# Attention and two feed-forward blocks in one launch: three of the four large products cut into 2x2 blocks and done in seven products, the norm moved ahead of its product, and the whole program ordered by a list scheduler

## The chip, the core and the metric

The kernel runs on one core of a Trainium2 chip. The core has a matrix engine (TensorE, PE in the tables; its weight loads are PEld), a vector engine (VectorE, DVE), a scalar engine (ScalarE, ACT), GpSimd (POOL), and a queue for DMAs (SyncE, SP). Each engine works through its own list of instructions in order and waits on semaphores for the others. Matrix products are gathered in PSUM, eight banks of 128 x 512 float32; the rest lies in SBUF. The metric is the device time in microseconds, a median over runs.

## The reference

```python
scores = scale * q @ k.T                      # 2 x 12 heads, 448 x 448, head size 64
attn   = softmax(where(causal, scores, -1e9))
x  = attn @ v                                 # 896 tokens x 768
h  = x @ w_in                                 # 768 x 2048            "in1"
g  = where(h >= 1, h, where(h <= -1, 0, (h + 1)**2 / 4))
y  = g @ w_out                                # 2048 x 768            "out1"
xn = y / sqrt(mean(y*y) + 1e-6) * rms_g       # per token
a  = silu(xn @ w_gate) * (xn @ w_val)         # 768 x 1536, twice     "gate/val"
return a @ w_out2                             # 1536 x 768            "out2"
```

The weights come as float64. The host passes them on as pairs of 32-bit words, and the kernel makes a float32 of each pair.

## The kernel before, in words

Everything is kept transposed: features on the 128 partitions, tokens along the columns. The 896 tokens are two batches of S = 448, and h = 0, 1 stands for the batch from in1 on. Attention works through 12 groups of two heads (`scores`, `maxima`, `exps`, `transposes`, `pv`, `xsplit`), with TensorE going through scores, transposes and PV products of neighbouring groups in turn.

Every operand of a large product is split into a high part (rounded to the matrix engine's fast 32-bit format) and a low part (the rest), and a product is three matmuls: high x high, high x low, low x high (`mm3`, L371; out1 at L564; out2 at L679). Each matmul is 128 x 128 weights by 128 x 448 tokens. So in1 is 16 column blocks x 2 batches x 6 x 3 = 576 matmuls, out1 576, gate/val 2 x 12 x 2 x 6 x 3 = 864, out2 6 x 2 x 12 x 3 = 432.

A weight block of 128 x 768 goes through a pipeline of steps: a DMA of 768 KB into one of three staging buffers (L139), a scaling on ScalarE (L174, `w_scale`), a shift, an `or` of the sign and a combining `or` on VectorE (L159, L165, L178), the high part on ScalarE (L184), the low part on GpSimd (L192). From the seventh block on the partial words lie in two PSUM banks. The paces at which these steps are put among the others are the six numbers of `RATE`; `w_need` forces what is due.

After in1, `moe_act` and `moe_min` (L379, L380, L384) make g. `gsplit` (L517, L518) splits it for out1, two blocks ahead. After out1, `rms_a` takes the six result blocks from PSUM: y times rms_g, split (L579, L581), and the squares (L580), summed (L584). The sum over features is a matmul against ones (L590), and the reciprocal root R follows (L591 to L601). The normalisation itself is done behind gate and val: their results are multiplied by R on the way out of PSUM (L642, L644), then SiLU (L643) and the product (L645), and `split` (L631, L632) for out2. The order of the instructions on every engine is that of the code, a schedule written by hand: while attention's last three units run, `push_in` and `pump` put two column blocks of in1 (36 matmuls) into the gaps.

```python
for k in ks:
    for n, (a, c) in enumerate(((0, 0), (0, 1), (1, 0))):
        nc.tensor.matmul(out, lhsT=w[:, a, k * P:(k + 1) * P], rhs=x[:, c, k], ...)   # L371
```

## Time and profile before

| | |
|---|---|
| time, median of 3 runs | 609.89 us (609.83 to 610.97) |
| span of the profiled execution | 607.9 us |
| between span and median | 2.0 us |
| busy: TensorE, VectorE, ScalarE, GpSimd | 594.1, 391.0, 281.9, 173.0 us |
| matmuls and transposes | 3124 |
| DMA | 67.8 MB, 112 GB/s over the span |

The span runs from the first to the last instruction of the profiled execution; the time of a run has some 2 us around it. Busy time is the sum of what an engine's instructions last. TensorE's matmuls overlap: one lasts about 0.37 us in the profile, and they start 0.2 us apart.

### The profile page before, as it was taken

How to read it: one execution, taken by the hardware profiler on the slowest of the kernel's cores; microseconds unless marked ns; L12 is line 12 of the kernel's file. 1: busy time of each engine (PE TensorE's matmuls, PEld its weight loads, DVE VectorE, ACT ScalarE, POOL GpSimd, SP SyncE). 2: the span in 40 equal slices, each digit the busy share in tenths (PEclk: the TensorE clock that was granted, in tenths of full speed). 3: DMA queues.
4: the chain of work that ended last, by engine and by line, in shares of the span. 5: the costliest groups of instructions: out<-in, count | busy, mean ns of one | idle time of the engine just before them, and what ended most of it. 6: DMA issues, size and time to landing. Idle time of an engine off the chain costs nothing.

```text
span 607.9 us, 8305 instructions
## 1 busy us (share of the span) xinstructions
PE 594.1 (98%) x3124; PEld 517.8 (85%) x3124; DVE 391.0 (64%) x643; ACT 281.9 (46%) x555; POOL 173.0 (28%) x118
## 2 busy tenths in 40 slices
PE   6999999899999999999999999999999999999997
PEld 4555558799999989998899999999999999999996
DVE  5678884378787646655594688877767766963100
ACT  5778775266676644345434433333333333543100
POOL 3446442234334413230122103322222222232200
PEclk9999999899999999999999999999999999999999
DMA  8454541234554423431132203333332333182100
GB/s 305 125 172 118 165 115 30 69 104 157 160 187 173 158 72 134 145 116 52 53 104 85 72 1 105 104 110 132 123 105 104 105 105 104 53 250 89 42 31 30
DMA packets 21495, 67.81 MB, mean 112 GB/s; under 512 B 5264, under 2 KB 11408, under 8 KB 21456
## 3 DMA queue, kind: packets, MB, share of 16 engines
q1 hardware_dynamic: 21456, 67.30, 34.1%
q8 instruction: 24, 0.39, 0.3%
q14 instruction: 15, 0.12, 0.1%
HBM read 64.49 MB, written 2.80 MB: 111 GB/s over the span
## 4 chain that ended last, share of the span: by engine, by line
PE 96%; DVE 1%; ACT 1%; issue 1%; DMA 0%; POOL 0%; SPq 0%; ACTq 0%; DVEq 0%
PE ps L371 48%; PE ps L564 18%; PE ps L679 14%; PE ps L278 7%; PE ps L309 4%; PE ps L352 4%; DMA af<-in_qT 0%; PE ps L590 0%; DVE ar L581 0%; ACT af L379 0%; ACT af L380 0%; ACT af L293 0%; DVE ps L165 0%; DVE af L178 0%; ACT af L327 0%
## 5 line engine op out<-in xcount | busy, mean ns | idle before, releaser
L371 PE MATMUL ps<-ar 128*128 128x448 f32 x1440 | 294.4, 367 | 0.0
L371 PEld LDWEIGHTS ps<-ar 128*128 128x128 f32 x1440 | 271.2, 189 | 22.0 <-issue 0.6
L192 POOL TENSOR_TENSOR ar<-af,ar 128x768 fp32r<-128x768 f32 x68 | 128.6, 1892 | 329.7 <-ACT ar L184 329.6
L564 PE MATMUL ps<-ar 128*128 128x448 f32 x576 | 118.1, 366 | 0.4 <-DVE ar L581 0.3
L564 PEld LDWEIGHTS ps<-ar 128*128 128x128 f32 x576 | 108.0, 188 | 10.2 <-DVE ar L581 0.9
L184 ACT CAST ar<-af 128x768 fp32r<-128x768 f32 x68 | 60.3, 887 | 99.1 <-DVE af L178 96.2
L679 PE MATMUL ps<-ar 128*128 128x448 f32 x432 | 87.7, 365 | 0.0
L679 PEld LDWEIGHTS ps<-ar 128*128 128x128 f32 x432 | 81.2, 188 | 6.4
L174 ACT ACTIVATE af<-af 128x768 f32<-128x768 f32 x62 | 56.6, 913 | 26.4 <-DMA af<-in_w_out 16.3
L165 DVE SCALAR_TENSOR_TENSOR ps<-af,ps 128x768 int32<-128x768 int32 x62 | 59.6, 961 | 12.2 <-ACT af L174 9.7
L159 DVE TENSOR_SCALAR ps<-af 128x768 int32<-128x768 int32 x62 | 59.1, 954 | 5.8 <-DMA af<-in_w_out 4.8
L178 DVE SCALAR_TENSOR_TENSOR af<-af,ps 128x768 int32<-128x768 int32 x62 | 59.2, 954 | 5.2
L293 ACT ACTIVATE af<-ps,nm 112x336 f32<-112x336 f32 (+2 forms) x96 | 47.0, 504 | 14.6 <-DVE nm L285 13.4
L285 DVE CUSTOM_DVE_ANT_0 ps<-ps,af 112x336 f32<-112x336 f32 (+2 forms) x96 | 41.8, 466 | 17.0 <-PE ps L278 16.0
L278 PE MATMUL ps<-af 64*112 64x448 f32 (+3 forms) x192 | 42.7, 444 | 7.1 <-DVE af L256 4.5
L518 DVE TENSOR_TENSOR ar<-af,ar 128x448 fp32r<-128x448 f32 x32 | 23.3, 732 | 40.3 <-ACT ar L517 40.3
L384 DVE SCALAR_TENSOR_TENSOR af<-af,ps 128x448 f32<-128x448 f32 x32 | 19.7, 618 | 40.3 <-ACT af L380 40.3
L517 ACT CAST ar<-af 128x448 fp32r<-128x448 f32 x32 | 18.0, 566 | 49.7 <-PE ps L564 49.7
L278 PEld LDWEIGHTS ps<-af 64*112 64x112 f32 x192 | 18.5, 179 | 22.5 <-ACT af L293 6.8
L379 ACT ACTIVATE af<-ps,half 128x448 f32<-128x448 f32 x32 | 20.2, 632 | 27.4 <-PE ps L371 24.9
L682 ACT COPY af<-ps 128x448 f32<-128x448 f32 x12 | 6.4, 533 | 53.4 <-PE ps L679 27.3
L644 DVE TENSOR_TENSOR af<-ps,af 128x448 f32<-128x448 f32 x24 | 14.9, 621 | 24.7 <-PE ps L371 24.7
(49 smaller groups left out, 393.5 us busy)
## 6 DMA issues: line engine op xcount, KB each, us to landing
af<-in_w_out SPq DMA_DIRECT2D x28, 768.0 KB, 4.3
af<-in_w_in SPq DMA_DIRECT2D x16, 768.0 KB, 4.4
af<-in_w_gate SPq DMA_DIRECT2D x12, 768.0 KB, 4.3
...
```

What stands on the lines that cost most here:

```text
L159: nc.vector.tensor_scalar(out=out, in0=t, scalar1=29, scalar2=0, op0=ALU.logical_shift_right, op1=ALU.bitwise_or)
L165: nc.vector.scalar_tensor_tensor(out=t, in0=words(n, 1, I32), scalar=-2 ** 31, in1=t, op0=ALU.bitwise_and, op1=ALU.bitwise_or)
L174: nc.scalar.mul(c, c, 2.0 ** -112)
L178: nc.vector.scalar_tensor_tensor(out=words(n, 0, I32), in0=words(n, 1, I32), scalar=3, in1=part.pop(n), op0=ALU.logical_shift_left, op1=AL ...
L184: nc.scalar.copy(dst[:, 0, :], value(n))
L192: nc.gpsimd.tensor_tensor(out=dst[:, 1, :], in0=value(n), in1=b32(dst[:, 0, :]), op=ALU.subtract)
L278: nc.tensor.matmul(bs[j][:C, o:o + (c + 1) * C], lhsT=q[r, c * C:(c + 1) * C], rhs=k[r, :(c + 1) * C], start=True, stop=True, skip_group_c ...
L285: nc.vector.tensor_tensor_reduce(out=t, in0=t, in1=mask[:C, S - (c + 1) * C:], scale=-1.0, scalar=3e38, op0=ALU.add, op1=ALU.min, accum_ou ...
L293: nc.scalar.activation(Pn[:C, j, poff[c]:poff[c] + w], sbank[n][j][:C, o:o + w], ACTF.Exp, bias=nm[:C, j, c:c + 1], scale=-1.0, accum_out= ...
L371: nc.tensor.matmul(out, lhsT=w[:, a, k * P:(k + 1) * P], rhs=x[:, c, k], start=(k == 0 and n == 0), stop=(k == NK - 1 and n == 2))
L564: nc.tensor.matmul(ybs[dm][:, :S], lhsT=w[:, a, dm * P:(dm + 1) * P], rhs=t[:, c], start=(n == 0 and i == 0), stop=(n == NM - 1 and i == 2))
L679: nc.tensor.matmul(ob[:, :S], lhsT=w2[dm][:, kk // NK, a, kk % NK], rhs=x[:, c], start=(kk == 0 and i == 0), stop=(kk == NF - 1 and i == 2))
```

## The change

**Seven products.** A product of 2x2 blocks needs eight block products. The change does in1, gate/val and out2 in seven, by mixing blocks first. In in1 and gate/val a group takes two weight blocks of 128 columns (`src1`, `src2`, block columns 1 and 2); the first and the second half of the 768 features are the block rows, and the two batches are the block columns of the tokens. Four mixed weights (`add(5)`, `add(6)`, `add(7)`, `add(3)`) and four mixed token blocks (`operand`) are formed in float32, then each of the seven is split into high and low. A group is 7 x 3 x 3 = 63 matmuls where it was 72. Partial sums are shared: a finished product is copied on ScalarE from its bank to a second bank, to which the next product adds (`seeds`), or, for the first groups, summed on VectorE (`sums`). out2 (`outer`) mixes the blocks of `a` and of w_out2 in the same way, with the seven products one after the other. out1 stays plain.

**Normalised first.** `y_out` takes y times rms_g out of PSUM unsplit; `normal` forms R as before and multiplies the tokens by it; only then are they mixed and split. Gate and val come out of PSUM with no factor.

**One scaling and sign step.** The scaling on ScalarE becomes a leaky form that leaves sign and exponent in place; VectorE's separate sign step is gone, and the shift stays in SBUF.

**Order.** Nothing is issued when it is described. Each operation goes into `Plan` with the engines that may do it, a duration on each, and what it reads and writes. `run` gives each a latest start, counted back from TensorE's sequence, and places them by that; an operation without a PSUM operand can go to VectorE or GpSimd, and one of VectorE marked as sharing with GpSimd is not placed beside one of GpSimd. TensorE's order is fixed by the code (`chain`). The table of durations (`act_t`, `dve_t`, `pool2_t`) sets the order; two of its entries stand below. Buffers are handed out from two arenas by which was freed first, and in the attention part at most two weight blocks are staged, later three.

```diff
+        order = sorted(range(n), key=lambda i: (lst[i], i))
+        lines = {e: [] for e in self.ENGINES}
...
+        self.start, self.end, self.eng = start, end, eng
+        for i in sorted(range(n), key=lambda i: (start[i], i)):
+            self.fn[i](eng[i])
+
+
+def act_t(n, bias=False):
+    return 0.03 + 0.001 * n + (0.06 if bias else 0.0)
+
+
+def dve_t(n):
+    return 0.07 + 0.00105 * n
...
-    def w_sign(n):
-        if wide:
-            t = part[n]
-            nc.vector.scalar_tensor_tensor(out=t, in0=words(n, 1, I32), scalar=-2 ** 31, in1=t,
-                                           op0=ALU.bitwise_and, op1=ALU.bitwise_or)
...
+        top = ("top", st.off, len(plan.alts))
+        low = ("low", st.off, len(plan.alts))
+        op({"ACT": act_t(n)},
+           lambda e: nc.scalar.activation(words(1, F32), words(1, F32), ACTF.Prelu, scale=2.0 ** -112,
+                                          alpha=-2.0 ** 32), [st], [top])
+        op({"DVE": (dve2_t(n), True)},
+           lambda e: nc.vector.tensor_scalar(out=words(0, I32), in0=words(0, I32), scalar1=29, scalar2=0,
+                                             op0=ALU.logical_shift_right, op1=ALU.bitwise_or), [st], [low])
...
+    def group(src1, src2, T, out, need, seeded, ps, rel=(0.0, 0.0), leads=(16, 10, 8)):
...
+        def mix_ps():
+            room([HW] * 4, W7)
+            w_float(st[0], True, None)
+            add(5, q(21), q(22), ALU.add)
+            raw(1)
+            add(6, me(5), q(11), ALU.subtract)
+            add(7, q(11), q(21), ALU.subtract)
+            raw(2)
+            add(3, q(12), me(6), ALU.subtract)
+            free(wf[1].sub(0, HW))
+            raw(4)
+            free(wf[1].sub(HW, HW))
+            for p in sorted(mixed, key=lambda p: need[p]):
+                split(W[p], mixed[p], HW)
+                free(mixed[p])
...
+        def seeds(p, o):
+            if p == 1:
+                bank_of["b"] = n = bank_take()
+                copy_op(bank(n), bank(o), S, [], [bk(o), bk(n)])
+            elif p == 6:
+                bank_of["e"] = n = bank_take()
+                copy_op(bank(n), bank(o), S, [], [bk(o), bk(n)])
+                tmp["u"] = u = SF.first(S, SHORT, ())
+                copy_op(ap(u), bank(o), S, [], [bk(o), u])
+            elif p == 7:
+                u = tmp["u"]
+                tt_op(ap(u), bank(o), ap(u), ALU.subtract, S, [], [bk(o), u], ps=True)
+            elif p == 5:
+                out(22, (o, tmp["u"]))
+                free(tmp["u"])
+            else:
+                out({2: 11, 4: 21, 3: 12}[p], (o, None))
+                bank_give(o)
+
...
+    def group_seq(n, lead_in):
+
+        if lead_in == 2:
+            s = [(0, 1), (1, 1), (0, 2), (1, 2), (0, 5), (1, 5), (0, 6), (1, 6), (0, 7), (1, 7), (0, 4), (1, 4),
+                 (0, 3)]
+            last = 1
+        else:
+            s = [(0, 1), (1, 1), (0, 2), (2, 1), (1, 2), (2, 2)] + [(g, p) for p in (5, 6, 7, 4, 3) for g in range(3)]
+            s.pop()
+            last = 2
+        for g in range(lead_in, n):
+            s += [(g, 1), (last, 3), (g, 6), (g, 2), (g, 7), (g, 5), (g, 4)]
+            last = g
+        return s + [(last, 3)]
...
+    def normal(b):
+        acc = rms[b][0]
+        o = 7
+        op({"PE": 0.95}, lambda e: nc.tensor.matmul(bank(o), lhsT=ap(ones), rhs=ap(acc), start=True, stop=True,
+                                                    skip_group_check=True), [acc, ones], [bk(o)], chain="PE", tail=0.15)
+        ms, rs, R = acc, SF.first(S, SHORT, ()), SF.first(S, SHORT, ())
+        op({"DVE": dve_t(S)}, lambda e: nc.vector.tensor_scalar(
+            out=ap(ms), in0=bank(o), scalar1=1.0 / (NK * P), scalar2=1e-6, op0=ALU.mult, op1=ALU.add), [bk(o)], [ms])
+        op({"ACT": act_t(S) + 1.3}, lambda e: nc.scalar.activation(ap(rs), ap(ms), ACTF.Sqrt), [ms], [rs])
+        for c in range(NCH):
+            x = rs.sub(c * C, C)
...
+            tt_op(ap(x), ap(x), ap(R), ALU.mult, S, [x, R], [x])
+        for p in ((1, 2), (5, 6, 7, 4, 3))[b]:
+            for k in range(HK):
+                ready.add((p, k))
```

The order on the engines, at three places. First TensorE, from the last PV product of attention to the end of the program. L352 and L852 are the PV products, L371 is in1 and gate/val, L564 out1, L590 the matmul against ones, L679 out2. Before:

```order
L352 MATMUL ps<-af 64x112 x2
L352 MATMUL ps<-af 64x336 x2
L352 MATMUL ps<-af 64x224 x2
L352 MATMUL ps<-af 64x112 x2
L371 MATMUL ps<-ar 128x448 x540
L564 MATMUL ps<-ar 128x448 x360
L590 MATMUL ps<-af,ones 128x448
L564 MATMUL ps<-ar 128x448 x216
L371 MATMUL ps<-ar 128x448 x36
L590 MATMUL ps<-af,ones 128x448
L371 MATMUL ps<-ar 128x448 x828
L679 MATMUL ps<-ar 128x448 x432
```

After (L491 in1 and gate/val, L1026 out1, L980 the matmul against ones, L561 out2):

```order
L852 MATMUL ps<-sf 64x112 x2
L491 MATMUL ps<-sr 128x448 x504
L1026 MATMUL ps<-sr 128x448 x306
L980 MATMUL ps<-sf 128x448
L1026 MATMUL ps<-sr 128x448 x270
L491 MATMUL ps<-sr 128x448 x9
L980 MATMUL ps<-sf 128x448
L491 MATMUL ps<-sr 128x448 x747
L561 MATMUL ps<-sr 128x448 x378
```

The rows of in1 have 504 matmuls in place of 540 and the 36 that stood ahead of this piece; gate/val 756 in place of 864; out2 378 in place of 432. The second matmul against ones has moved from behind 36 matmuls of gate/val to behind 9.

Second VectorE, at the head of gate/val, from the mean of the second batch's squares (L591 before, L983 after) on. Before (L642, L644 and L645 take gate and val out of PSUM; L596 is the reciprocal; L599 to L601 finish R):

```order
L591 TENSOR_SCALAR af<-ps 128x448
L642 TENSOR_TENSOR af<-ps,af 128x448
L644 TENSOR_TENSOR af<-ps,af 128x448
L645 TENSOR_TENSOR af<-af 128x448
L632 TENSOR_TENSOR ar<-af,ar 128x448
L596 RECIPROCAL af<-af 128x112 x4
L599 TENSOR_TENSOR af<-af 128x448
L600 SCALAR_TENSOR_TENSOR af<-af 128x448
L601 SCALAR_TENSOR_TENSOR af<-af 128x448
L642 TENSOR_TENSOR af<-ps,af 128x448
L644 TENSOR_TENSOR af<-ps,af 128x448
```

After (L304 is every two-input operation: `sf` and `sr` are the SBUF arenas, `ps` is PSUM; an output in `sr` is a low part; L349 is the shift of the words):

```order
L983 TENSOR_SCALAR sf<-ps 128x448
L304 TENSOR_TENSOR sr<-sf,sr 128x384
L304 TENSOR_TENSOR sf<-ps,sf 128x384
L304 TENSOR_TENSOR sr<-sf,sr 128x384
L349 TENSOR_SCALAR sf<-sf 128x768
L988 RECIPROCAL sf<-sf 128x112 x4
L304 TENSOR_TENSOR sf<-sf 128x448
L990 SCALAR_TENSOR_TENSOR sf<-sf 128x448
L992 SCALAR_TENSOR_TENSOR sf<-sf 128x448
L304 TENSOR_TENSOR sf<-sf 128x448 x5
L304 TENSOR_TENSOR sr<-sf,sr 128x448
```

Between the matmul against ones and the first low part of the second batch's tokens there now stand the mean, four reciprocals, R, and the products with R on VectorE; before, R was needed only behind the products, on the way out of PSUM.

Third VectorE in the middle of gate/val. Before, two weight blocks' worth of rows (L159, L165 and L178 are the steps of the words):

```order
L159 TENSOR_SCALAR ps<-af 128x768
L165 SCALAR_TENSOR_TENSOR ps<-af,ps 128x768
L178 SCALAR_TENSOR_TENSOR af<-af,ps 128x768
L642 TENSOR_TENSOR af<-ps,af 128x448
L644 TENSOR_TENSOR af<-ps,af 128x448
L645 TENSOR_TENSOR af<-af 128x448
L632 TENSOR_TENSOR ar<-af,ar 128x448
L159 TENSOR_SCALAR ps<-af 128x768
L165 SCALAR_TENSOR_TENSOR ps<-af,ps 128x768
L178 SCALAR_TENSOR_TENSOR af<-af,ps 128x768
```

After (L349 and L359 are the steps of the words):

```order
L304 TENSOR_TENSOR sr<-ps,sr 128x384
L304 TENSOR_TENSOR sf<-sf 128x384
L304 TENSOR_TENSOR sf<-sf,ps 128x384
L304 TENSOR_TENSOR sf<-ps,sf 128x448 x2
L304 TENSOR_TENSOR sr<-ps,sr 128x384
L304 TENSOR_TENSOR sf<-ps,sf 128x448
L349 TENSOR_SCALAR sf<-sf 128x768
L304 TENSOR_TENSOR sf<-ps,sf 128x448
L304 TENSOR_TENSOR sf<-ps,sf 128x384
L359 SCALAR_TENSOR_TENSOR sf<-sf 128x768
L304 TENSOR_TENSOR sr<-sf,sr 128x384
```

Operations of 384 columns, many of them with both inputs in SBUF, have come between the steps of the words, and the low parts of the weights, which GpSimd made before, stand on VectorE.

## Rows read from the trace of the kernel before

**Rows 1.** The page: busy time, share of the span, instructions by engine.
```profile
PE 594.1 (98%) x3124; PEld 517.8 (85%) x3124; DVE 391.0 (64%) x643; ACT 281.9 (46%) x555; POOL 173.0 (28%) x118
```

**Rows 2.** Windows: length; busy PE, PEld, DVE, ACT, POOL; granted clock, DMA share, GB/s.
```profile
0.00:95.00 95.00, 87.93 (x620) 52.62 (x620) 73.18 (x244) 69.99 (x229) 42.50 (x46) 1.00 0.53 163
...
98.80:221.60 122.80, 121.05 (x601) 110.91 (x601) 78.26 (x97) 69.71 (x105) 43.98 (x25) 0.99 0.39 131
221.60:341.00 119.40, 118.37 (x579) 108.23 (x578) 74.98 (x95) 53.36 (x82) 28.25 (x15) 1.00 0.28 93
341.00:517.00 176.00, 176.00 (x869) 162.83 (x868) 130.57 (x165) 61.30 (x91) 40.28 (x22) 1.00 0.30 99
517.00:604.50 87.50, 87.44 (x432) 80.72 (x430) 32.10 (x39) 23.23 (x38) 16.25 (x9) 1.00 0.26 83
```

**Rows 3.** The chain that ended last, after attention: start, us, what.
```profile
110.82 110.76 PE ps L371 x540
...
296.26 1.02 PE ps L590 x2
297.27 43.77 PE ps L564 x216
...
348.34 0.75 PE ps L590 x2
349.09 167.80 PE ps L371 x828
516.89 87.57 PE ps L679 x432
604.52 0.53 ACT af L682
```

**Rows 4.** Timeline at the end of attention: start, us, instruction, [idle before, releaser].
```profile
108.25 2.57 PE L352 MATMUL ps<-af 112*64 112x336 f32 x20 [1.75 <-ACT af L327]
```

**Rows 5.** Groups by shape: line engine op, shapes, count, busy us, mean ns, idle before.
```profile
L184 ACT CAST ar<-af 128x768 fp32r<-128x768 f32 x68 | 60.3, 887 | 99.1 <-DVE af L178 96.2 <-PE ps L371 2.9
L178 DVE SCALAR_TENSOR_TENSOR af<-af,ps 128x768 int32<-128x768 int32 x62 | 59.2, 954 | 5.2
L174 ACT ACTIVATE af<-af 128x768 f32<-128x768 f32 x62 | 56.6, 913 | 26.4 <-DMA af<-in_w_out 16.3 <-DMA af<-in_w_in 10.0
L645 DVE TENSOR_TENSOR af<-af 128x448 f32<-128x448 f32 x24 | 25.5, 1064 | 5.2 <-ACT af L643 3.4
L327 ACT COPY af<-ps 112x448 f32<-112x448 f32 x48 | 24.1, 537 | 9.0 <-PE ps L309 9.0
L644 DVE TENSOR_TENSOR af<-ps,af 128x448 f32<-128x448 f32 x24 | 14.9, 621 | 24.7 <-PE ps L371 24.7
L631 ACT CAST ar<-af 128x448 fp32r<-128x448 f32 x24 | 12.6, 564 | 26.7 <-DVE af L645 26.7
```

**Rows 6.** Single lines: count, duration least/median/greatest in ns, first and last start.
```profile
L159 DVE TENSOR_SCALAR af<-af x4: 543/558/566, 11.1 to 81.1; 128x768 int32<-128x768 int32 x4
L364 POOL TENSOR_TENSOR ar<-af,ar x12: 1127/1930/2342, 25.0 to 119.8; 128x448 fp32r<-128x448 f32 x12
L192 POOL TENSOR_TENSOR ar<-af,ar x68: 1857/1885/2398, 27.4 to 569.4; 128x768 fp32r<-128x768 f32 x68
L645 DVE TENSOR_TENSOR af<-af x24: 624/931/1931, 352.3 to 522.4; 128x448 f32<-128x448 f32 x24
```

**Rows 7.** Timeline in gate/val: start, us, instruction, [idle before, releaser].
```profile
349.67 0.61 DVE L642 TENSOR_TENSOR af<-ps,af 128x448 f32<-128x448 f32 x1
350.20 0.61 DVE L644 TENSOR_TENSOR af<-ps,af 128x448 f32<-128x448 f32 x1
...
354.09 2.98 DVE L596 RECIPROCAL af<-af 128x112 f32<-128x112 f32 x4
...
365.03 1.88 POOL L192 TENSOR_TENSOR ar<-af,ar 128x768 fp32r<-128x768 f32 x1 [25.16 <-ACT ar L184]
...
365.46 1.92 DVE L645 TENSOR_TENSOR af<-af 128x448 f32<-128x448 f32 x1 [0.43 <-ACT af L643]
```

More of the change, by code (lines that the diff above doesn't have):

```diff
@@ new lines, with ap, free, bank @@
+    plan = Plan()
+    op = plan.op
+    E = {"PE": nc.tensor, "ACT": nc.scalar, "DVE": nc.vector, "POOL": nc.gpsimd, "SP": nc.sync}
+    def ap(b, dtype=None):
+        t = b.space.tile[:, b.off:b.off + b.n]
+        return t if dtype is None else t.bitcast(dtype)
+    def free(*bufs):
+        for b in bufs:
+            b.space.free(b)
+    def bank(i):
+        return pst[:, i, :S]
+    def bk(i):
+        return BANK + i
+    ident = SF.alloc(P)
+    ones = SF.alloc(P)
+    half = SF.alloc(1)
@@ new lines, with bank_take, bank_give, copy_op @@
+    gvec = SF.alloc(NK)
+    stats = [SF.alloc(3 * 2 * NCH) for _ in range(4)]
+    bfree = {i: 0 for i in range(8)}
+    bclock = [0]
+    def bank_take():
+        i = min(bfree, key=lambda i: bfree[i])
+        del bfree[i]
+        return i
+    def bank_give(i):
+        bclock[0] += 1
+        bfree[i] = bclock[0]
+    def copy_op(dst, src, n, r, w, **kw):
+        op({"ACT": act_t(n)}, lambda e: nc.scalar.copy(dst, src), r, w, **kw)
+    def tt_op(dst, a, b, alu, n, r, w, ps=False, pool=True, **kw):
+        alts = {"DVE": (dve_t(n), not ps)}
+        if not ps and pool:
+            alts["POOL"] = pool2_t(n)
+        op(alts, lambda e: E[e].tensor_tensor(out=dst, in0=a, in1=b, op=alu), r, w, **kw)
@@ L367, in mm3 @@
-    def mm3(out, w, x, ks=None):
-        ks = range(NK) if ks is None else ks
-        for k in ks:
-            for n, (a, c) in enumerate(((0, 0), (0, 1), (1, 0))):
-                nc.tensor.matmul(out, lhsT=w[:, a, k * P:(k + 1) * P], rhs=x[:, c, k],
-                                 start=(k == 0 and n == 0), stop=(k == NK - 1 and n == 2))
-    ntmp = [0]
-    def moe_act(m, h, ps):
-        u = tmp[ntmp[0] % 2]
-        ntmp[0] += 1
-        nc.scalar.activation(u, ps, ACTF.Relu, bias=half, scale=0.5)
-        nc.scalar.activation(u, u, ACTF.Square)
-        gate.append((m, h, ps, u))
@@ new lines, with moe_out, out @@
+    half_a = ap(half)
+    def moe_out(G, j):
+        def out(qn, src):
+            o, t = src
+            g = G[qn, j] = SF.first(S, LONG, ())
+            u = SF.first(S, SHORT, ())
+            h, hk = bank(o), bk(o)
+            if t is not None:
+                tt_op(ap(g), h, ap(t), ALU.add, S, [t], [hk, g], ps=True)
+                h, hk = ap(g), g
+            op({"ACT": act_t(S, True)},
+               lambda e: nc.scalar.activation(ap(u), h, ACTF.Relu, bias=half_a, scale=0.5), [], [hk, u])
+            op({"ACT": act_t(S)}, lambda e: nc.scalar.activation(ap(u), ap(u), ACTF.Square), [u], [u])
+            op({"DVE": (dve_t(S), t is not None)}, lambda e: nc.vector.scalar_tensor_tensor(
+                out=ap(g), in0=ap(u), scalar=1.0, in1=h, op0=ALU.min, op1=ALU.max), [u], [hk, g])
+            free(u)
+        return out
@@ new lines, in val_out, with out @@
+    def val_out(j):
+        def out(qn, src):
+            o, u = src
+            t = A[qn, j] = sil[qn, j]
+            if u is not None:
+                h = SF.alloc(S)
+                tt_op(ap(h), bank(o), ap(u), ALU.add, S, [u], [bk(o), h], ps=True)
+                tt_op(ap(t), ap(h), ap(t), ALU.mult, S, [h, t], [t])
+                free(h)
+            else:
+                tt_op(ap(t), bank(o), ap(t), ALU.mult, S, [t], [bk(o), t], ps=True)
+        return out
+    NL = NF // 2
+    srcs, outs = [], []
@@ L685 @@
+    emit_preps(-3, 5)
+    free(*held)
+    staged[1] = 3
+    for i in range(6):
+        bank_give(i)
+    for i, f in enumerate(units):
+        now[0] = i
+        while later and later[0][0] <= i:
+            later.pop(0)[1]()
+        emit_preps(i, i)
+        f()
+    body = tc.manual_schedule()
+    body.__enter__()
+    plan.run()
     body.__exit__(None, None, None)
@@ L700, with words @@
     wide = w_in.dtype == np.float64
+    def words(w):
+        return w.view(np.int64) if wide else w
     def blocks(w):
[L703 to L704 removed]
+        w = words(w)
         K, N = w.shape
```

1241 lines of the change are left out of this document (810 added, 431 removed).

## The prediction

> **What bounds the kernel now.** I read the busy shares first, then the stages in a table of windows, then the chain that ended last. TensorE is busy 594.1 of 607.9 us, VectorE 391.0, ScalarE 281.9 [rows 1]. In the table of windows TensorE fills every stage after attention (121.05 of 122.80 us, 118.37 of 119.40, 176.00 of 176.00, 87.44 of 87.50), while VectorE has 122.80 - 78.26, 119.40 - 74.98, 176.00 - 130.57 and 87.50 - 32.10 us to spare [rows 2]. The chain says the same in order of time: long unbroken pieces of matmul and hardly anything between [rows 3]. A busy TensorE need not be one at its best, so I take its pace from the chain: 828 matmuls in 167.80 us, 432 in 87.57, 216 in 43.77 are 202.7, 202.7 and 202.6 ns each; the first 540 took 110.76 us, 205.1 ns each, in a stretch whose windows show the granted clock at 0.99 [rows 2, 3]. So today the time is the number of matmuls times 202.7 ns, plus attention, plus the end. Any change in it must come from fewer matmuls or from a new wait of TensorE.
>
> The span is 607.9 us and the median of the runs 609.89, so 2.0 us lie around the span; I sum against the span and add the 2.0 at the end.
>
> **What the change removes.** The listed order of TensorE has 2448 matmuls of 128x448 before (576 + 36 + 828 in the blocks that share L371, 576 in out1, 432 in out2) and 2214 after (504 in in1, 576 in out1, 756 in gate/val, 378 in out2). That the change does what it says is thereby settled before any run: 234 fewer, times 202.7 ns, are 47.4 us. Attention's matmuls and transposes are the same, in the same order.
>
> The sum from the left: in1 works unbroken from 110.82 us on and had put 36 matmuls into gaps of attention before that [rows 3], so without them it would stand at 110.82 - 36 x 0.2027 = 103.5 us. These 36 covered waits: the last PV product waited 1.75 us for a copy on ScalarE [rows 4], behind in1's own Relu and Square. After the change nothing of in1 stands there, TensorE waits in the open, but the copy also comes sooner; I take 103.5, from 102.5 to 105.5. Then 2214 x 0.2027 = 448.8 us; two matmuls against the ones for the norm, 1.02 + 0.75 = 1.8 [rows 3]; the end from the last matmul to the end of the span, 607.9 - 604.5 = 3.4, unchanged but for a VectorE subtraction in place of a ScalarE copy. That is 557.5 us with no new wait. The same reckoning for the kernel before gives 103.5 + 2448 x 0.2027 + 1.8 + 3.4 = 604.9, so it has 3.0 us of waits and clock; they are the measure of what a good order loses.
>
> **What it adds.** Each product of the seven needs its own weights and tokens, mixed by additions and split into a high and a low part. The pieces are 384 columns wide in place of 768, a width that the trace does not have. A VectorE operation takes 0.621 us at 448 columns and 0.954 at 768 [rows 5], a straight line between them gives 0.55 at 384; the bounds are 0.53 (in proportion) and 0.62. ScalarE takes 0.564 at 448 and 0.887 at 768, so 0.50 at 384 (0.48 to 0.564). GpSimd's two-input form at its quickest takes 1.127 us at 448 and 1.857 at 768 [rows 6], so 0.98 at 384; its slowest at 448 columns, 2.342, is the upper end. Copies from one PSUM bank to another, which seed the later products, are priced as a copy out of PSUM, 0.537 [rows 5] (up to 0.954, what an operation of 768 columns takes). The new way to turn the 64-bit words into floats saves a pass: one ScalarE operation as before (0.913), a shift that now stays in SBUF (0.558 instead of 0.954 [rows 5, 6]) and one combination (0.954): 68 times 0.954 + 0.40 less on VectorE.
>
> VectorE in all, counted from the listed order: 250 operations of 384 columns at 0.55, 282 of 448 at 0.62, 15 and 68 of 768 at 0.95, 68 shifts at 0.56, 6 us of reciprocals, and attention's own, some 75 (73.2 in its first 95 us [rows 2], with its weight passes taken off and its last group put on): 137 + 175 + 79 + 38 + 6 + 75 = 510 us. That is 91% of 558 us where it was 64%. ScalarE comes to about 435 us, 78%. These are durations; two neighbours that don't wait for each other start 0.53 us apart where each lasts 0.61 to 0.62 [rows 7], so VectorE's need is some 0.08 us less for each of these 680 or so operations, about 455 us.
>
> By stage, because the mean means little. In in1, TensorE needs 504 x 0.2027 = 102.2 us; VectorE has 174 operations in that part of its order, 106.9 us by durations and 93 by starts; ScalarE 98 and 82. In gate/val a group of two weight blocks is 63 matmuls, 12.8 us, and VectorE needs for it 2 shifts, 2 combinations, 11 operations of 384 and 4 of 448 columns on average: 11.5 by durations, 10.1 by starts. In out2 it is 94 and 82 us against 76.6 us of TensorE, but a fifth of these stand in gate/val's time. Out1 has slack. So TensorE stays the bound if VectorE's queue runs as in [rows 7], and VectorE is late by up to 5 us in in1 if every duration counts in full. The order is one fixed list per engine, and a late operation holds all behind it on its engine; what protects TensorE is that weights are made 8 to 16 products ahead.
>
> The new waits that I can place: (1) The norm of the second batch. Its matmul against the ones runs one product after out1, and then five products (45 matmuls, 9.1 us) need only the first batch. The chain is 0.62 on VectorE for the mean, 0.56 on ScalarE for the root, 2.98 for four reciprocals [rows 7], and nine more operations of 448 columns at 0.62 until the first low part of the second batch's tokens is there, 9.7 us: TensorE waits about 1 us (0 to 3; the scalar engine's table for the root is still loaded from the first batch). (2) In out2 the banks of the first product are copied before the next product may add to them: three blocks of 0.61 us on TensorE, two copies each on ScalarE at up to 0.54 us, of which the next product needs the first: about 1 us (0 to 2). (3) The clock, 1 us, as in in1 before. (4) Lateness in in1 and at the head of gate/val, 1 to 2 us. All of it: 557.5 + 1 + 1 + 1 + 1.5 = 562 us, with the 2.0 around it 564 us. The DMA load is the same 68 weight blocks of 768 KB; at a share of 0.26 to 0.39 [rows 2] I cost it at nothing.
>
> The trace shows one thing against the change. The product at L645, both inputs in SBUF, takes 0.624 us at its quickest and 1.92 where GpSimd's subtraction had begun 0.43 us before it [rows 6, 7]; 356 of VectorE's new additions and subtractions have both inputs in SBUF. The rule behind it stands in the Trainium skill, page SBUF — State Buffer, section "Who interferes with whom": a VectorE instruction with two SBUF inputs contends with a GpSimd instruction that reads SBUF. By that rule VectorE could lose, as an estimate, up to 66 x 0.98 = 65 us to GpSimd's 66 two-input operations, all of it inside its queue; by a mean of the quickest rows alone it loses nothing. The trace agrees with the rule where the two meet, and I price the meeting from L645 below.
>
> **The rivals.**
> Nothing waits: 557.5 + 2.0 = 559.5 us. For it: the gaps between an engine's operations in the trace are short when a neighbour has other work. Against: the kernel before lost 3 us with a far emptier VectorE.
>
> VectorE is the bound in two stages: by durations in1 needs 106.9, and each of its some 12 GpSimd subtractions may hold VectorE 0.5 us, 113 in place of 102.2; out2 has four fifths of 94, 75 of its 76.6 us, so that the meetings with some 15 GpSimd operations there and at the end of gate/val, 0.4 us each, come through: 6. With the 1 to 3 us of the norm that is 559.5 + 11 + 6 + 2 = 578 us. For it: 106.9 > 102.2. Against: the starts 0.53 us apart.
>
> Slower: VectorE stands at every split. A split is a cast on ScalarE and then a subtraction on VectorE. If each of a group's seven subtractions stood 0.43 us and was stretched by 0.44, as L645 is (its mean is 1.064 against 0.624 at its quickest [rows 5, 6]; the 0.43 is the idle time in [rows 7]), a group would take 11.5 + 7 x 0.87 = 17.6 us of VectorE. With 26 such groups (8 in in1, 12 in gate/val, 6 steps of out2), 26 x 17.6 + 103.5 + 118 + 3.4 + 2.0 = 685 us. It decides from 12.8 + 9 x 0.2027 = 14.6 us a group on, 3.1 more than I count: there the seven products cost what eight did. For it: L645 shows both. Against: GpSimd has only 66 two-input operations left where it had 80, at 0.98 in place of 1.9 us, so stretching has some 65 us in all to give; and the new order puts operations on other tiles between a cast and its subtraction.
>
> **How the numbers follow.** 564 us has 0.60 (its own range 560.5 to 569), nothing waits 0.15, VectorE the bound in two stages 0.20, slower 0.05. The range from 558 to 578 leaves out the slower case, the tail above 578 and a little below. Within 0.2% of the time before (1.2 us, what a measurement of this kernel can tell from no change) only a mixture of half the slower case would come: 0.01. Faster 0.94, slower 0.05.
>
> **What would show it.** Right: TensorE's chain in four long pieces of about 102, 118, 154 and 77 us at 203 to 205 ns a matmul; VectorE near 85 to 93% busy, the wait list with no more than 6 us of TensorE waiting behind VectorE and ScalarE after attention; a wait of about 1 us of TensorE behind VectorE some 11 us after out1's last matmul, and behind it the reciprocals and products of the norm. Wrong: matmuls at 215 ns or more in in1 or out2 with VectorE at 98%; two-input VectorE operations with a mean above 0.8 us; a granted clock under 0.95 in a stage. The forecast falls if TensorE's idle time after attention is over 15 us.

## The result, and the profile after

The changed kernel takes 571.36 us (median of 4 runs: 571.67, 571.9, 571.05 and 566.78), the kernel before 609.86: a ratio of 0.9355, 95% interval 0.9319 to 0.9391. The forecast was 564.0, with a range of 558 to 578: faster as forecast, 7.4 us above the point. The profiled run took 571.67 us, its span 570.0.

The page's busy time of after, the answer to [rows 1]:

```profile
PE 552.1 (97%) x2890; PEld 475.1 (83%) x2890; DVE 476.5 (84%) x932; ACT 377.5 (66%) x807; POOL 89.5 (16%) x86
```

TensorE has 234 matmuls less and is still the fullest engine; VectorE went from 391.0 to 476.5 us, under the 510 that the durations gave.

The chain that ended last, against [rows 3] (start, us, what; the pieces between 320.20 and 330.00 are short ones of ScalarE and VectorE):

```profile
102.88 51.28 PE ps L491 x252
...
185.59 20.74 PE ps L491 x99
206.32 63.24 PE ps L1026 x306
...
270.32 49.86 PE ps L1026 x246
...
330.00 1.86 PE ps L980 x2
331.86 11.09 PE ps L491 x45
...
345.76 63.04 PE ps L491 x302
...
421.72 67.76 PE ps L491 x333
489.47 76.92 PE ps L561 x378
```

In1 (L491) starts at 102.88 and takes 103.4 us, 205 ns a matmul; out2's 378 take 76.92, 203.5 ns each. One place is bad: between the end of out1 (324.87, where the next matmul starts) and 345.76. There 45 matmuls take 11.09 us, 246 ns each. The waits of TensorE (in all, times, longest) behind attention, and windows of 5 us over that place (columns as in [rows 2]):

```profile
PE ps L980 <- DVE sf L304: 3.1, 1, 3.1
...
PE ps L491 <- ACT sr L298: 1.1, 1, 1.1
```

```profile
325.00:330.00 5.00, 1.85 (x10) 1.37 (x9) 5.00 (x9) 3.76 (x9) 1.03 (x1) 0.92 0.89 291
330.00:335.00 5.00, 5.00 (x11) 3.82 (x12) 4.44 (x9) 2.64 (x6) 0.00 (x0) 0.50 0.06 23
335.00:340.00 5.00, 5.00 (x24) 4.60 (x23) 4.83 (x7) 4.12 (x6) 1.99 (x2) 0.90 0.00 0
...
345.00:350.00 5.00, 4.80 (x16) 3.84 (x15) 4.91 (x9) 1.13 (x2) 1.46 (x1) 0.66 0.00 0
```

L980 is the matmul of the second batch's squares against the ones. TensorE stands 3.1 us for it; then the granted clock is 0.50 (1.2 of 2.4 GHz) for 5 us, with 11 matmuls where 24 fit, and 0.66 once more at 345. A busy share of 5.00 out of 5.00 hides that.

VectorE's list there shows why (the timeline of VectorE, and below it GpSimd's):

```profile
325.73 0.95 DVE L359 SCALAR_TENSOR_TENSOR ps<-sf 128x768 int32<-128x768 int32 x1
326.60 1.41 DVE L304 TENSOR_TENSOR sf<-sf 128x448 f32<-128x448 f32 x1
327.94 0.54 DVE L304 TENSOR_TENSOR sf<-sf,ps 128x384 f32<-128x384 f32 x1
328.40 0.61 DVE L304 TENSOR_TENSOR sf<-sf 128x448 f32<-128x448 f32 x1
328.94 0.54 DVE L304 TENSOR_TENSOR sr<-ps,sr 128x384 fp32r<-128x384 f32 x1
329.41 0.54 DVE L304 TENSOR_TENSOR sf<-ps,sf 128x384 f32<-128x384 f32 x1
...
331.90 0.62 DVE L983 TENSOR_SCALAR sf<-ps 128x448 f32<-128x448 f32 x1 [0.56 <-PE ps L980]
332.44 0.55 DVE L304 TENSOR_TENSOR sr<-sf,sr 128x384 fp32r<-128x384 f32 x1
...
334.31 2.98 DVE L988 RECIPROCAL sf<-sf 128x112 f32<-128x112 f32 x4
337.39 1.42 DVE L304 TENSOR_TENSOR sf<-sf 128x448 f32<-128x448 f32 x1
...
340.17 2.77 DVE L304 TENSOR_TENSOR sf<-sf 128x448 f32<-128x448 f32 x5
344.00 0.63 DVE L304 TENSOR_TENSOR sr<-sf,sr 128x448 fp32r<-128x448 f32 x1 [1.07 <-ACT sr L298]
```

```profile
326.50 1.03 POOL L304 TENSOR_TENSOR sr<-sf,sr 128x384 fp32r<-128x384 f32 x1 [1.57 <-ACT sr L298]
336.34 1.99 POOL L304 TENSOR_TENSOR sr<-sf,sr 128x384 fp32r<-128x384 f32 x2 [8.80 <-ACT sr L298]
```

The last two additions of squares (326.60 and 328.40, 448 columns) stand behind and between weight preparation and end at 329.01. L980 writes bank 7, which the subtraction of 329.41 still reads, to 329.95; at 330.00 it starts. Two operations beside a working GpSimd take 1.41 and 1.42 us in place of 0.62. From 324.87 to the first split of the new tokens, the subtraction at 344.00, it is 19.1 us. TensorE has work for 11.7 of them (54 matmuls and the ones), so 7.4 us are lost to this chain.

To compare kernels, the loss of each stage: its length by the starts of its matmuls in the trace, less 202.7 ns for each. The table has one profiled execution of each kernel; "in1 from" is in1's start in the chain. A slow piece of attention moves the start of in1 by up to 4.6 us from one run to the next (e1: granted clock 0.73 from 30 to 40 us, in1 from 107.5), so medians a few us apart say less than this table. The kernel before, measured beside each group of runs, took 609.8 us (e1 to e4), 612.8 (e5 to e10) and 609.9 (e11 to e14), so medians of different groups may be off by some 3 us as well. The stretch "norm" is the first 75 matmuls behind out1; a mark in "bank" says that batch 2's ones-matmul has one of its own.

| kernel | median us | bank | in1 from | in1 | out1 | norm | rest of gate/val | out2 |
|---|---|---|---|---|---|---|---|---|
| after | 571.4 | | 102.9 | 1.2 | 1.5 | 10.4 | 0.4 | 0.3 |
| e1_bank | 575.8 | x | 107.5 | 0.3 | 0.3 | 2.7 | 5.9 | 4.0 |
| e2_nowait | 572.9 | x | 103.0 | 0.9 | 1.5 | 0.7 | 6.4 | 4.0 |
| e4_shift | 586.0 | | 106.3 | 5.2 | 0.3 | 7.6 | 7.3 | 5.1 |
| e5_eight | 616.4 | | 103.5 | 0.1 | 1.4 | 7.0 | 1.1 | 0.3 |
| e7_sqrt | 575.0 | x | 103.6 | 0.3 | 0.3 | 2.2 | 8.3 | 3.4 |
| e9_noshift | 568.1 | | 103.8 | 0.1 | 0.3 | 8.1 | 0.2 | 0.3 |
| e10_neither | 566.3 | x | 103.7 | 0.1 | 0.3 | 0.3 | 4.4 | 3.5 |
| e11_rsqrt | 569.1 | | 104.5 | 0.2 | 1.4 | 4.8 | 1.2 | 0.3 |
| e12_dummy | 582.3 | x | 103.8 | 2.1 | 1.5 | 0.4 | 7.1 | 4.1 |
| e13_lead | 570.1 | | 103.7 | 0.4 | 0.3 | 6.5 | 1.8 | 0.1 |
| e14_light | 564.7 | | 103.8 | 0.1 | 0.3 | 3.0 | 1.8 | 0.3 |

### The profile page after: what moved, and what is told of

The parts are those of the page before. It is cut to its first block, busy times and chain, and to the rows that moved or that the text cites. A ratio compares the mean times of both kernels' runs of the same rounds, so it can differ in the third digit from the quotient of the medians.

```text
span 570.0 us, 8284 instructions
## 1 busy us (share of the span) xinstructions
PE 552.1 (97%) x2890; PEld 475.1 (83%) x2890; DVE 476.5 (84%) x932; ACT 377.5 (66%) x807; POOL 89.5 (16%) x86
## 4 chain that ended last, share of the span: by engine, by line
PE 86%; DVE 6%; DMA 3%; ACT 3%; issue 1%; POOL 0%; SPq 0%; DVEq 0%; ACTq 0%
PE ps L491 38%; PE ps L1026 20%; PE ps L561 13%; PE ps L763 7%; PE ps L799 4%; PE ps L852 4%; DVE sf L304 2%; DMA sf<-in_w_in 1%; DVE sr L304 1%; DMA sf<-in_w_gate 1%; ACT sr L298 1%; DVE sf L359 1%; DVE sf L349 1%; DMA sf<-in_qT 0%; DVE ps L359 0%
## 5 line engine op out<-in xcount | busy, mean ns | idle before, releaser
L491 PE MATMUL ps<-sr 128*128 128x448 f32 x1260 | 262.2, 370 | 1.8 <-ACT sr L298 1.1
L491 PEld LDWEIGHTS ps<-sr 128*128 128x128 f32 x1260 | 239.0, 190 | 24.7 <-ACT sr L298 1.9
L298 ACT CAST sr<-sf 128x384 fp32r<-128x384 f32 (+2 forms) x260 | 137.4, 557 | 81.7 <-DVE sf L304 28.0
L304 DVE TENSOR_TENSOR sr<-sf,sr 128x448 fp32r<-128x448 f32 (+2 forms) x218 | 131.5, 628 | 23.4 <-ACT sr L298 19.0
L1026 PE MATMUL ps<-sr 128*128 128x448 f32 x576 | 118.6, 367 | 0.0
L1026 PEld LDWEIGHTS ps<-sr 128*128 128x128 f32 x576 | 108.2, 188 | 10.1 <-issue 0.4
L304 POOL TENSOR_TENSOR sr<-sf,sr 128x384 fp32r<-128x384 f32 (+2 forms) x42 | 53.0, 1267 | 304.8 <-ACT sr L298 298.0
L304 DVE TENSOR_TENSOR sf<-ps,sf 128x448 f32<-128x448 f32 (+1 forms) x113 | 66.4, 597 | 14.5 <-PE ps L491 7.8
L561 PE MATMUL ps<-sr 128*128 128x448 f32 x378 | 77.1, 366 | 0.0
L561 PEld LDWEIGHTS ps<-sr 128*128 128x128 f32 x378 | 70.8, 188 | 6.2 <-ACT ps L298 0.4
L304 DVE TENSOR_TENSOR sf<-sf 128x448 f32<-128x448 f32 (+1 forms) x88 | 56.0, 663 | 19.0 <-ACT sf L964 18.7
L346 ACT ACTIVATE sf<-sf 128x768 f32<-128x768 f32 x68 | 62.0, 922 | 8.0 <-DMA sf<-in_w_in 2.4
L780 ACT ACTIVATE sf<-ps,sf 112x336 f32<-112x336 f32 (+2 forms) x96 | 47.3, 509 | 6.9 <-DVE sf L771 6.0
L359 DVE SCALAR_TENSOR_TENSOR sf<-sf 128x768 int32<-128x768 int32 x50 | 48.3, 975 | 1.4 <-ACT sf L346 0.4
L304 POOL TENSOR_TENSOR sf<-sf 128x448 f32<-128x448 f32 (+1 forms) x24 | 29.2, 1226 | 88.1 <-DVE sf L304 52.5
L349 DVE TENSOR_SCALAR sf<-sf 128x768 int32<-128x768 int32 x68 | 41.0, 609 | 2.3 <-DMA sf<-in_w_in 0.9
L304 DVE TENSOR_TENSOR sr<-ps,sr 128x384 fp32r<-128x384 f32 (+1 forms) x54 | 30.1, 560 | 3.9 <-ACT sr L298 3.1
```

The source lines that it names most:

```text
L298: op({"ACT": act_t(n)}, lambda e: nc.scalar.copy(dst, src), r, w, **kw)
L304: op(alts, lambda e: E[e].tensor_tensor(out=dst, in0=a, in1=b, op=alu), r, w, **kw)
L346: lambda e: nc.scalar.activation(words(1, F32), words(1, F32), ACTF.Prelu, scale=2.0 ** -112, alpha=-2.0 ** 32), [st], [top])
L349: lambda e: nc.vector.tensor_scalar(out=words(0, I32), in0=words(0, I32), scalar1=29, scalar2=0, op0=ALU.logical_shift_right, op1=ALU.bitw ...
L359: nc.vector.scalar_tensor_tensor(out=out, in0=hi, scalar=3, in1=lo, op0=ALU.logical_shift_left, op1=ALU.bitwise_or)
L491: nc.tensor.matmul(bank(o), lhsT=ap(d.sub(x * HW + k * P, P)), rhs=ap(t.sub(y * S, S)), start=(begin and k == 0 and i == 0), stop=(k == HK ...
```

## The experiments

**e1_bank, e2_nowait: take the wait away.**

```diff
-        o = 7
+        o = bank_take() if b else 7        # e1, e2; given back behind L983
-            tt_op(ap(x), ap(x), ap(R), ALU.mult, S, [x, R], [x])
+            tt_op(ap(z), ap(x), ap(R), ALU.mult, S, [x, R], [z])    # e2, batch 2: z is thrown away
```

> The ones-matmul of batch 2 gets a PSUM bank of its own instead of bank 7, which weight preparation still reads in the changed kernel when that matmul could start (the last reading addition ends 329.95 us, the matmul starts 330.00, after 3.15 us in which TensorE stood). Theory A (the missing time lies at this transition: TensorE stands there, the granted clock falls to 0.50, and the rest runs at 203 to 205 ns a matmul): the wait ahead of the ones-matmul falls from 3.1 us to at most 2.2, because the last addition of the squares ends 329.01 and the bank is then free; if the clock stays up as well, up to 5 us more come back: 566 to 571 us. Rival (the order of VectorE's queue sets it, the bank is only seen last): wait 2.2 us or more, clock still 0.50, time 570 to 572.

> As the one before, and the tokens of batch 2 go into the products without their factor (the multiplication is still done, into a scratch buffer; the normalisation of batch 2 is left out of the result). So no product waits for the chain of the norm. Theory A: both waits of TensorE at the transition are gone, the granted clock stays at 1.0, and the time falls by 9 to 10 us, to 561.5 to 563.5. Rival B (VectorE is what bounds gate/val and out2; the waits at the transition only show it first): the time falls by less than 4 us, to 567.5 or more, with other waits behind VectorE later.

Measured: 575.81 us (574.76 to 576.89) and 572.86 (571.27 to 575.6). In both the wait at L980 is gone and the clock is 1.00 behind out1; in e2 TensorE works through (against 15.57 busy of 20.00 us in after):

```profile
324.70:345.00 20.30, 20.23 (x98) 18.13 (x97) 20.11 (x33) 12.61 (x24) 4.08 (x3) 1.00 0.00 0
```

So the bank and the plan behind it do make L980 late. The bank alone is 0.9 us of it, from 329.01 to 329.95 in after. The rest is the plan: freed from bank 7, it puts the additions of squares ahead of the weight work, and in e1 the last one ends 1.4 us after out1's end (327.42), where in after it was 4.1:

```profile
328.20 0.63 DVE L304 TENSOR_TENSOR sf<-sf 128x448 f32<-128x448 f32 x1 [0.34 <-ACT sf L964]
```

But the time did not fall: 9.9 and 10.4 us are lost later, where after lost 0.7. e1's median lies above the ranges of both its readings; from in1's start to the end it takes 466.6 us, where after takes 467.1. By its numbers e2 spoke for rival B, and I took it for the reading that VectorE bounds there and has to be given a lead. That is what e12 tried, below.

**e3_order: the program's order.**

```diff
-        for i in sorted(range(n), key=lambda i: (start[i], i)):
+        for i in range(n):
```

> The instructions of every engine are issued in the order in which the program writes them, not by their planned start; products, engines and buffers as in the changed kernel. This prices the part 'whole program put in order by deadlines'. If the order carries much of the gain, each preparation stands where the program writes it, ahead of or behind work that is due sooner, and TensorE waits at many places: 590 us or more. If the order hardly matters (the program is already written with leads of 5 to 16 units): 571 to 576. [...]

Measured: 792.74 us (791.65 to 793.47), a ratio to before of 1.300 (1.2975 to 1.3026). That is the first of the two cases, 200 us beyond its bound: the order by planned start is worth 221 us to this program as it is written. TensorE waits at dozens of places, and its mean granted clock is 0.874:

```profile
PE ps L491 <- DVE sf L304: 37.3, 10, 6.7
PE ps L491 <- ACT sr L298: 26.6, 9, 3.5
PE ps L561 <- ACT ps L298: 20.6, 2, 10.8
PE ps L491 <- ACT sf L298: 20.3, 3, 13.5
PE ps L980 <- DVE sf L304: 18.7, 1, 18.7
```

**e4_shift, e5_eight: more work for one engine.**

```diff
-  nc.vector.tensor_scalar(..., scalar1=29, ...)
+  [nc.vector.tensor_scalar(..., scalar1=k, ...) for k in (29, 0)]                  # e4
+  for _ in range(2 if p == 7 else 1): op({"PE": 3 * MM}, fn, ...)                 # e5
```

> Behind each VectorE shift of the weight decoding stands a second one by 0 bits, of which the planner knows nothing: 68 more of some 0.55 to 0.6 us, so 37 to 41 us more on VectorE (476 to 515 us of the span), in all four stages. Theory A (TensorE is the bound; VectorE is 85 to 91% busy in the stages, so it has 8 to 10% to spare): part of it is hidden; VectorE then wants 94.1 + 10 of 103 us in in1, 62.9 + 6 of 69.5 in gate/val, 69.7 + 8 of 77 in out2, so it is just full there and the time rises by 2 to 12 us. Rival B (VectorE already bounds): the time rises by nearly all of it, 30 to 40 us, to over 600.

> In in1, gate/val and out2 the matmuls of the seventh product are issued twice (its sums come out wrong for that): 72 + 108 + 54 = 234 more, the 234 that the change took out, 47.4 us at 202.7 ns, and nothing more for any other engine. If TensorE is the bound everywhere after the attention, apart from one wait at the norm (the reading before the last runs), the time rises by all of it: 571.4 + 47 = 618 to 619. If VectorE bounds from the end of out1 on (what the runs without the waits at the norm point to: from the start of in1 to the end they took 466.6 and 466.7 us against 467.1), TensorE has some 10 us to spare there, and only in1's 14.6 us and 22 to 25 of the other 32.8 are paid: 607 to 611.

Measured: e4 585.99 us (583.38 to 591.14). The shifts take 79.7 us instead of 41.0:

```profile
L349 DVE TENSOR_SCALAR sf<-sf 128x768 int32<-128x768 int32 x136 | 79.7, 589 | 7.3 <-DMA sf<-in_w_out 2.0 <-DMA sf<-in_w_in 1.5 <-DMA sf<-in_w_gate 1.4
```

By the medians 14.6 of these 38.7 us are paid; 11.6 lie behind in1's start (478.7 us to the end, where after took 467.1), in in1, gate/val and out2; out1 hides its share. VectorE isn't the bound, but it has little to spare in three of four stages. e5 616.41 us (614.36 to 618.18): 45.1 of 47.4 us are paid by the medians, 43.5 from in1's start to the end, where the norm loses 3.4 less than in after; so TensorE bounds nearly everywhere. The edit is not quite clean: the planner knows of the added matmuls and gives GpSimd 21 instructions more than in after (107 for 86). My 607 to 611 was wrong, and with it the 10 us that TensorE was to have to spare.

**e7_sqrt, e9_noshift, e10_neither: a shorter chain, a lighter VectorE.**

```diff
-        op({"ACT": act_t(S) + 1.3}, ... Sqrt ...)
+        op({"ACT": act_t(S)}, ... Sqrt ...)                                         # e7, with e1's bank
-  nc.vector.tensor_scalar(... logical_shift_right ...)                              # e9, and e10 on e2
-  nc.vector.scalar_tensor_tensor(out=out, in0=hi, scalar=3, in1=lo, ...)
+  nc.vector.tensor_scalar(out=out, in0=hi, scalar1=3, scalar2=0, ...)
```

> The ones-matmul of batch 2 with a bank of its own, and the planner's duration of the square root cut from 1.78 us to 0.48 (the trace of the changed kernel has 0.58), so that the chain of the norm is planned 1.3 us shorter. An attempt at a better version. If the norm's chain is what costs: 1.3 to 4 us less than the run with the bank alone from the start of in1 to the end (462 to 465 against 466.6). If VectorE bounds whatever stands first in its queue: the same 466 to 467.

> The weight decoding leaves out the lowest three bits of every weight: no shift of the low words, and the step that joins the words becomes an operation with one input. Nothing is told to the planner, so the order stays. VectorE has 68 shifts of 0.61 us less and 68 joins that are perhaps 0.4 us shorter: 40 to 67 us of its 476.5. If VectorE bounds from out1's end on: the waits at the norm shrink and none take their place, 560 to 564 (from the start of in1 to the end 456 to 460 instead of 467.1). If it is the latency of the norm's chain alone: VectorE's part of the chain stays, and 567 to 571.

> Both: the tokens of batch 2 without their factor (as in the run without the wait, which leaves out that normalisation), and the lighter weight decoding (lowest three bits left out). If VectorE's work is what took the place of the wait in that run, TensorE now waits for nothing: 2214 matmuls at 202.7 ns, two ones-matmuls and the end, 448.8 + 1.8 + 3.4 = 454 us from the start of in1, so 455 to 458 and 559 to 562 in all (less if the attention ends earlier too). If something else held that run back (transfers of weights, which showed in its chain of waits with some 20 us, or the room for them), it stays at 463 or more.

Measured: 575.02 us (573.15 to 580.16), 568.06 (567.02 to 572.71), 566.29 (564.25 to 568.04). From in1's start to the end e7 takes 467.8 us, above both of its readings: a chain that is only planned shorter gained nothing. e9's median lies in its second reading, the latency of the chain; its 462.2 us from in1's start are above the 456 to 460 of the first. VectorE falls to 421.9 us in e9. Without the bank it loses 8.1 at the norm and nothing later; with it and without the wait (e10) it loses nothing at the norm and 7.9 later, with VectorE as light. So VectorE's load alone does not decide where the later waits come; e10 ended 461.9 us from in1's start, neither the 455 to 458 of its first reading nor the 463 of its second; whether transfers of weights held it back was not tested.

**e11_rsqrt to e14_light: a better version, and the lead.**

```diff
-        op({"ACT": act_t(S) + 1.3}, ... ACTF.Sqrt ...)                              # e11, e13, e14
-        for c in range(NCH): ... nc.vector.reciprocal(ap(x), ap(x)) ...
+        op({"ACT": act_t(S)}, ... ACTF.Abs_reciprocal_sqrt ...)
+            for i in range(48 if b else 0): nc.tensor.matmul(bank(o), ...)          # e12, on e2, ahead of L980
-    outer(NL, ..., split_last=3)
+    outer(NL, ..., leads=(15, 11, 8), split_last=3)                                 # e13, on e11
```

> An attempt at a better version: in the norm ScalarE's square root and VectorE's four reciprocals become one ScalarE reciprocal square root (the two polishing steps behind it stay), for both batches; the bank stays shared. The chain of batch 2 loses four reciprocals of 0.745 us = 3.0 us, VectorE 6.0 us of work, and the planner no longer counts 1.3 us too much for the root. All by the time from the start of in1 to the end of the span, 467.1 in the changed kernel. If the latency of the chain is what costs: the 10.5 us lost around the norm become 6 to 7, nothing else changes: 463 to 464, 567 to 568 in all. If VectorE's work bounds from out1's end on, TensorE gets ahead of it by as much and waits later: only some of VectorE's 3 us there come back: 464.5 to 467, 569 to 571.

> The run without the wait at the norm (tokens of batch 2 without their factor), and ahead of its ones-matmul 48 matmuls whose sums are thrown away, of which the planner knows nothing: 48 x 202.7 ns = 9.7 us of TensorE at a place where that run lost nothing. If the lead of VectorE over TensorE is what counts (that run lost 5.7 us of stalls in gate/val and 3.3 in out2, the changed kernel 0.4 and 0.3, after it had stood 10.5 us at the norm): the 48 matmuls do what the wait did, the later stalls go, and the time hardly rises: 466 to 469 us from the start of in1 (466.7 without them), 571 to 574. If those later stalls come from that kernel's other order and bank, each of the 48 is paid: 475 to 477, 580 to 582.

> The version with the reciprocal square root, and in out2 weights and tokens may be prepared 8 units ahead of their matmuls instead of 5 (loads and decoding 15 and 11 instead of 12 and 8). If VectorE is held back by how far ahead it may work, out2's stalls go where there are any and TensorE's earlier arrival is kept: 1 to 3 us less than the version before it. If VectorE is simply full: the same within 1 us.

> The reciprocal square root, and the lighter weight decoding (lowest three bits of each weight left out) of the earlier run, which took 462.2 us from the start of in1 to the end and lost 8.3 at the norm. VectorE has 420 us of work in place of 476. If the chain's latency is what costs at the norm, 3 to 4.3 us of the 8.3 go and with so light a VectorE nothing takes their place: 458 to 459, 562 to 563 in all. If single steps of gate/val and out2 want more of VectorE than of TensorE even so (out2's sixth product, which decodes nothing): 460 to 462, 564 to 566.

Measured: e11 569.11 us (567.54 to 575.16; ratio to before 0.9337, 0.9294 to 0.9379), e12 582.33 (579.31 to 585.34), e13 570.14 (566.21 to 573.87), e14 564.68 (564.34 to 571.26; 0.9274, 0.9231 to 0.9317).

e12 falls on the rival's number: 9.7 us of useless matmuls are paid in full and the later losses stay, 7.1 and 4.1. So TensorE's delay alone does not take the later losses away. But e12 does not decide the lead theory, that VectorE has to be given time, because it gave VectorE none: from 326.5 to 346 VectorE has 10.52 us of work in e12, where in e2 it had 20.11, since its own list waits at the mean (L983 before) for the ones-matmul behind the 48 (the second row):

```profile
326.50:346.00 19.50, 19.50 (x95) 17.63 (x94) 10.52 (x16) 7.54 (x17) 2.81 (x2) 1.00 0.00 0
```

```profile
339.21 0.62 DVE L989 TENSOR_SCALAR sf<-ps 128x448 f32<-128x448 f32 x1 [5.51 <-PE ps L986]
```

Against the lead speaks e10, where VectorE has 422.3 us of work in place of 476.5 and 7.9 us are lost later all the same.

e11 is the other half. L980 stands 2.56 us where in after it stood 3.15, the chain behind it has no reciprocals, and TensorE runs on where after stood 1.1 us:

```profile
329.98 1.86 PE L980 MATMUL ps<-sf 128*128 128x448 f32 x2 [2.56 <-DVE sf L304]
330.96 22.26 PE L491 MATMUL ps<-sr 128*128 128x448 f32 x101
```

The norm's loss goes from 10.4 to 4.8 us, gate/val and out2 rise by 0.8 only, so this gain is kept: the chain theory was right here. Not all of the 5.6 us is the chain. e13 has the same norm and lost 6.5 there, with a granted clock of 0.86 from 325 to 350 us where e11 had 0.93; and both were planned anew, so the order of their lists differs from after's too. In the medians it is 2.3 us, with intervals that overlap: in1 began 1.7 us later in e11's profile, and its runs lie up to 7.6 us apart. e13's longer lead gives nothing that can be measured. e14 is the fastest, 6.7 us under the changed kernel, with an interval that lies just below that kernel's; from in1's start it takes 458.7 us, its first reading. It gives up the lowest three bits of each weight. Of those that keep them all, e11 has the lowest median.

What e1, e2, e7, e10 and e12 share is the bank, so a chain planned earlier and another order of all lists behind it. Out2, from its first matmul to its last, in after, e1, e2, e11 and e14 (columns as in [rows 2]):

```profile
489.30:566.50 77.20, 77.08 (x379) 70.56 (x377) 69.87 (x128) 43.42 (x88) 8.57 (x4) 1.00 0.23 81
```

```profile
489.70:570.50 80.80, 79.80 (x379) 70.35 (x378) 72.50 (x132) 45.44 (x92) 9.21 (x5) 1.00 0.23 79
```

```profile
485.40:566.20 80.80, 80.24 (x379) 70.27 (x377) 73.47 (x133) 45.21 (x89) 8.53 (x4) 1.00 0.23 79
```

```profile
485.00:562.20 77.20, 77.11 (x380) 70.61 (x378) 69.90 (x129) 43.30 (x88) 8.56 (x4) 1.00 0.23 81
```

```profile
481.80:559.00 77.20, 77.11 (x380) 70.62 (x378) 64.48 (x121) 42.57 (x87) 8.21 (x4) 1.00 0.23 80
```

In e1 and e2 VectorE still has four or five instructions more to do when out2 begins; at some 0.56 us each these are 2.2 to 2.8 of the 3.6 us by which out2 is longer. Nor is it that TensorE came early: counted from in1's start, out2 begins after 382.2 us in e1 and after 380.5 in e11, which loses 0.3 there. That the place in the list does it, and not the bank as such, fits all twelve rows, but no run changed the order alone; that stays open, and so do gate/val's 4.4 to 8.3.

## Why the prediction was right, and where it was off

The mechanism was right: TensorE stays the bound, the time falls by the matmuls that are gone, and the one new wait that counts is at the norm. That 571.4 lies in the range is in part luck: the range reached to 578 for VectorE as a bound, which did not come, and the reading that had 0.60 ended at 569.

**The removal, right.** 234 matmuls at 202.7 ns; e5 puts them back and pays 45.1 us of the 47.4 by the medians.

**In1's start, the pace, the end, right.** 102.9 for 103.5; 448.8 us for 2214 matmuls, of which in1, out1, the rest of gate/val and out2 lost 3.4 in after; 4 us from out2's last matmul's start to the end for 3.4 from its end.

**The new wait (1) and the clock (3), too small by some 8 us.** They were 1 us each; the norm lost 10.4. The failed step is "the chain is [...] 9.7 us": it begins at the mean and adds durations as if VectorE's queue held nothing else. By the rows: the additions of squares ended 4.1 us after out1's end, one operation of each engine behind which should be some 1.5; bank 7 cost 0.9; the ones-matmul at half clock lasted 1.86 in place of 0.75; the reciprocals started 1.2 us after the root's end, behind weight work; one product beside GpSimd took 0.8 longer; and the first split stood 1.1 us for its cast on ScalarE (344.00), a step that the sum left out though it knew that a split begins with one. Of the five operations behind R (340.17), which the sum had counted, that split needs two by the code, a product with R and a subtraction. My sum had the queue in [rows 7], and the list of VectorE, shown ahead of it, has four operations between the mean and the reciprocals; it used neither.

The clock was priced from in1 of the kernel before, where it stood at 0.50 once, for some 3.4 us. What it costs here can only be estimated. Of the 10.4 us the chain takes some 7.4 (19.1 less 11.7), and some 3 are lost behind it. The slow matmuls ahead of 336 cost little by themselves, because TensorE then still stood 1.1 us for the split. The slow ones-matmul is 1.1 us in the chain, of which VectorE's queue hid about half (it stood 0.56 us ahead of the mean, 331.90). The stretch of 0.50 behind 346.3 lasts some 3.4 us and costs half of that. The one run of after whose granted clock was 1.000 throughout took 566.78, 4.6 under the median; it has no trace. Nor does the length of a wait tell, in these runs, whether the clock falls. In e4 TensorE stood 3.8 us for the ones-matmul and the clock stayed at 1.00; in e14 it stood 2.1 us and it stayed, in e9 also 2.1 and it fell to 0.50. e4 (the wait, and windows over and behind it):

```profile
PE ps L981 <- DVE sf L304: 3.8, 1, 3.8
```

```profile
330.00:340.00 10.00, 6.25 (x29) 5.17 (x28) 9.96 (x18) 7.69 (x16) 2.17 (x2) 1.00 0.43 157
340.00:350.00 10.00, 7.92 (x38) 6.70 (x37) 9.76 (x18) 5.53 (x10) 2.23 (x2) 1.00 0.00 1
```

**Seed copies (2) and lateness (4).** In1's 1.2 and gate/val's 0.4 fit (4). Out2's 0.3 us leaves nothing of the 1 us for (2).

**Rivals.** VectorE as a bound (0.20) did not come: in in1 and gate/val it is 91 to 94% full by the rows below (out2, above, 91%), and the 10 us lost were elsewhere. e4 shows how near it was.

```profile
103.00:206.00 103.00, 102.85 (x504) 94.12 (x504) 94.12 (x163) 82.06 (x154) 14.60 (x11) 1.00 0.38 128
...
350.00:420.00 70.00, 70.00 (x348) 64.88 (x347) 65.73 (x109) 41.35 (x78) 22.08 (x18) 1.00 0.36 125
420.00:489.50 69.50, 69.33 (x342) 63.93 (x341) 62.91 (x109) 46.44 (x90) 7.31 (x6) 1.00 0.40 140
```

VectorE standing at each split did not come: no shape of its additions and subtractions (L304) has a mean above 0.8 us at 384 or 448 columns. GpSimd's price can now be read, against the same width with an input in PSUM (groups by shape of after):

```profile
L304 DVE TENSOR_TENSOR sf<-ps,sf 128x448 f32<-128x448 f32 x77 | 47.4, 620 | 14.3 <-PE ps L491 7.8 <-PE ps L561 5.6
...
L304 DVE TENSOR_TENSOR sf<-sf 128x448 f32<-128x448 f32 x56 | 37.8, 698 | 19.0 <-ACT sf L964 18.7
```

That is 78 ns x 56 = 4.4 us here, and with 34 ns on 104 splits and 51 on 32 additions of 384 columns 9.5 in all, of the up to 65 that the prediction left room for. Where the two meet (326.60 above) it is a factor of 2.3. Of the 56 in the second row, nine ran beside a two-input operation of GpSimd and have a mean of 1.11 us, the other 47 one of 0.62; of the 77 in the first row 21 did, and none of them lasted over 0.63. This agrees with the rule of the Trainium skill (page SBUF — State Buffer, section "Who interferes with whom") that a VectorE instruction with two SBUF inputs contends with a GpSimd instruction that reads SBUF.

Of the signs named, the 15 us of idle TensorE did not come (4.8 after attention), and the wait at the norm did, longer than forecast, with the fall of the clock behind it.
